# A linear-attention and feed-forward kernel on one core: later units start one item later, and the third unit's scans go between the first scores and the first row

## The chip, the cores and the metric

One core of a Trainium2 chip. Time is device microseconds (us) of one execution; the figure compared is the median over runs. Engines: TensorE (PE, with its weight loads as PEld), VectorE (DVE), ScalarE (ACT), GpSimd (POOL), and SyncE (SP), which issues the DMAs. A line such as L600 is a line of the kernel.

## The reference

Gated linear attention over 768 time steps for 4 batches of 8 heads of 48 channels, then a feed-forward layer on the 3072 tokens it yields. The weights come as float64, the rest as float32; the output is float32.

```python
state = np.zeros((B, H, D, D), dtype=np.float32)          # B, H, S, D = 4, 8, 768, 48
for t in range(S):
    state = alpha[:, :, t, :, None] * state + np.einsum('bhd,bhe->bhde', k[:, :, t], v[:, :, t])
    y[:, :, t] = np.einsum('bhd,bhde->bhe', q[:, :, t], state)
...
x = y.transpose(0, 2, 1, 3).reshape(B * S, H * D)         # 3072 x 384
h = x @ w_in                                              # 384 x 2048
g = np.maximum(0.01 * h, h)
return (g @ w_out).astype(np.float32)                     # 2048 x 384
```

## The kernel before

**Attention.** Time is cut into 6 chunks of 128 steps; a *unit* is one chunk of one batch, with all 8 heads (24 units, numbered 0 to 23). Per unit: `scans` turns alpha on VectorE (`e`, a transpose), takes running products along time (`up`, four scans), their reciprocals at every 16th step and a backward scan (`down`); `scaled_q` and `scaled_k` turn q and k and multiply them by these (`qs`, `ks`); `sum_up` sums the absolute values of `up` and `down` on ScalarE. Then on TensorE: `scores` (ks against qs, L465 a<-qs,ks), `past` (state against qs, L465 a or ph<-qs,small), `values` (masked scores against v, L465 <-sm,small), `products` (new state, L465 a<-small,ktok), and `k_tokens` (four transposes, L398). `mask_scores` copies one half of the scores to `sm` on ScalarE (L384) and masks it on POOL, the other half is masked on VectorE; `split` writes the result as a high and a low float32r part into `large`; `next_state` updates the state.

**Feed-forward.** Three units make a block of 384 tokens, so there are 8 blocks i. The hidden width is cut into 16 tiles f. An *item* n is a pair (i, f); items 0 to 31 alternate between blocks 0 and 1 (item 2f + i), and from item 32 the blocks 2 to 7 follow one after another, 16 items each. I write in(n) for the first product of item n (`ffn_in`, nine matmuls into a PSUM tile `ph`, L600) and out(n) for its second (`ffn_out`, nine matmuls into `a` or `b`, L629). out(n) is issued behind in(n+3). Between them stand t(n), the scaled copy on ScalarE (L605) and the maximum on VectorE (L608); gh(n), a rounded copy on ScalarE (L610); gl(n), the rest, on VectorE (L614). The weights come as 64-bit words; during items 0 to 28 `converting` makes each of the 16 weight tiles w0 to w15 (a high and a low part) with six VectorE steps and two on ScalarE.

**What sets the order.** A scheduler places instructions by their order in the program and by its own estimate; three things bind it. VectorE's and ScalarE's work on items and on units from 9 on is chained in the order of emission (`put`). Each matmul emitted by `multiply` with `row`, and each product once `row` is set, is chained to the last one (`in_row`). And PSUM and SBUF buffers are reused as the scheduler hands them out, so that a matmul can wait for whoever read its bank last.

**The two phases.** `attention` does units 0 to 8 at the start. Units 9 to 23 are the *later units*: `attention_later` is a generator of steps, and `pace` advances it while the items run, twice per item (a call before and one after t): each call adds `slices` to `due` and emits steps until `emitted` has reached it. A unit's preparation has 7 steps: e; the four scans; reciprocal and backward scan; q turned; qs; k turned; ks. *row(u)* is the chained group past(u), scores(u+1), values(u), products(u); with mask, split, state and a unit's preparation a unit has 11 steps. Steps 1 to 28 are the start (units 9 and 10, of 11 the preparation). Step 15 (14 emitted) is held back while block 1's sums still stand in PSUM.

Items in the trace: at 149.07 us TensorE starts out(27), behind in(29); at 167.56 us in(35), at 195.79 us row(10).

Of the kernel before, what the change touches and what calls it, by code (L numbers as in the profile page):

```python
# [23 lines left out]
def gated_linear_attn_ffn(ctx, tc, q, k, v, alpha, w_in, w_out, out):  # L24
# [9 lines left out]
    NF = DF // P  # L34
# [25 lines left out]
    LAG = 3  # L60
    SOON, EARLY = 2, 3
    SL = 11 * UPB
    FIRST, LEAD = 29, 14


    kinds = ["a", "b"]
# [1 line left out]
    def bank(tag=None):  # L68
        if tag is None:
            tag = kinds[0]  # L70
            kinds.append(kinds.pop(0))
        return ps_x.tile([P, 512], F32, name=tag)
# [205 lines left out]
    def banks4():  # L278
        return bank().rearrange("r (p n) -> r p n", p=NP)
# [86 lines left out]
    def scores(u):  # L366

        pe, qs, ks = live[u]
        ss = [banks4(), banks4()]
        M = C if u < AHEAD else HB  # L370
        for p in range(NP):
            for s, lo in ((0, 0), (1, HB)):
                for t in range(0, C, M):
                    yield ss[s][t:t + M, p, :], ks[lo:lo + D, p, t:t + M], qs[lo:lo + D, p, :], True, True
        live[u].append(ss)
# [36 lines left out]
    def past(u):  # L412

        tb, b = units[u]
        qs, W = live[u][1], state[b].rearrange("r p n -> r (p n)")
        if u < AHEAD:
            y = banks4()
            ys[u] = [y[:, s::2, :] for s in (0, 1)], y
        else:
            first = bank()  # L420
            full = [first, ps_h.tile([P, 512], F32, name="ph")]
            ys[u] = [t[:, 0:2 * C].rearrange("r (p n) -> r p n", p=2) for t in full], first[:, 2 * C:2 * C + NP * D]
        if tb:
            for q, s, lo, top, p, at in heads():
                r = slice(0, BR) if u < AHEAD else slice(lo, lo + D)
                c, m = p * BR + lo, D if top else HB
                yield ys[u][0][s][at:at + m, q, :], W[r, c:c + m], qs[r, p, :], q == 0 and (s == 0 or u >= AHEAD), False

    def values(u):

        tb, b = units[u]
        V = vals_sb[u % NV]
        for q, s, lo, top, p, at in heads():
            c = (2 * p + s) * D
            m = D if top else HB
            yield (
                ys[u][0][s][at:at + m, q, :], V[:, c:c + m], masked[u][s][:, p, :],
                not tb and q == 0 and s == 0, q == 1 and (s == 1 or u >= AHEAD),
            )
        del masked[u]  # L440

    def products(u):

        tb, b = units[u]
        pe, qs, ktok = live[u][:3]
        V = vals_sb[u % NV]
        kv = None
        if tb < NC - 1:
            kv = ys[u][1] if u >= AHEAD else bank()[:, 0:NP * D]
            kv = kv.rearrange("d (p e) -> d p e", p=NP)  # L450
            for p in range(NP):
                for s, lo, m in ((0, 0, HB), (1, HB, D)):
                    h = 2 * p + s
                    yield kv[lo:lo + m, p, :], ktok[:, p, lo:lo + m], V[:, h * D:(h + 1) * D], True, True
        load_values(u + NV)
        live[u] = pe, kv

    row = []

    def multiply(groups, row=None):  # L460

        for group in groups:
            for out, weights, moving, start, stop in group:
                with tc.issue_after(row[-1].ins) if row else nullcontext():
                    made["product",] = nc.tensor.matmul(out, weights, moving, start=start, stop=stop, skip_group_check=True)  # L465
                if row is not None:
                    row[:] = [made["product",]]
# [79 lines left out]

    def attention_later(first, last):

        def prepared(u, at=None):  # L550

            if u < last:
                yield from chain(scans(u), scaled_q(u), scaled_k(u))
                sum_up(u)

        yield from prepared(first)
        for u in range(first - 1, last):
            new, old = u + 1 < last, u >= first
            next_one = prepared(u + 2)
            if not old:  # L560
                yield from next_one
            groups = [past(u)] if old else []
            if new:
                groups.append(scores(u + 1))
            if old:
                groups += [values(u), products(u)]
            multiply(groups, row)
            yield
            if old:
                yield from islice(next_one, 1)  # L570
                split(u)
                if u % UPB == UPB - 1:
                    gather(u // UPB)
                    ready.add(u // UPB)
                yield
            if new:
                mask_scores(u + 1)
                yield
            if old:
                next_state(u)  # L580
            if new:
                k_tokens(u + 1)
            yield
            yield from next_one

    def in_row():

# [2 lines left out]
    def ffn_in(i, f, steps=None):  # L590

        ordered = steps is not None
        first, second = steps or ((), ())
        xh, xl = xs[i]
        ph = ps_h.tile([P, 512], F32, name="ph")[:, 0:TB]
        n = 0
        with in_row():
            for g in range(NG):
                for wn, xt in ((HIGH, xh), (HIGH, xl), (LOW, xh)):
                    product = nc.tensor.matmul(ph, w_in_of(f, wn, g), xt[:, g, :], start=n == 0, stop=n == 3 * NG - 1)  # L600
                    n += 1
        if row or i > 1:
            row[:] = [product]
        t = ffp.tile([P, TB], F32, name="t")
        put(ordered, "ACT", lambda: nc.scalar.mul(t, ph, 0.01))  # L605
        for step in first:
            next(step, None)
        put(ordered, "DVE", lambda: nc.vector.tensor_tensor(t, ph, t, ALU.max))  # L608
        gh = ffp.tile([P, TB], F32R, name="gh", bufs=LAG + 1)
        put(ordered, "ACT", lambda: nc.scalar.copy(gh, t))  # L610
        for step in second:
            next(step, None)
        gl = ffp.tile([P, TB], F32R, name="gl", bufs=LAG + 1)
        made["gl", i, f] = put(ordered, "DVE", lambda: nc.vector.tensor_tensor(gl, t, gh.bitcast(F32), ALU.subtract))  # L614
        return gh, gl
# [49 lines left out]
    for n, _ in enumerate(st):  # L665
        if n == 2:
            load_values(NV - 1)
        while LOADS and LOADS[0][0] in made:
            key, f, part = LOADS.pop(0)
# [3 lines left out]
        u = AHEAD - EARLY + converted  # L673
# [4 lines left out]
        if n in STARTS:  # L678
            i, f = items[len(gs)][:2]
# [5 lines left out]
    due, emitted = 0.0, 0  # L685
    new = coming = None
    later_units = attention_later(AHEAD, NU)

    def pace(slices):

        nonlocal due, emitted
        while True:
            due += slices
            while emitted < due and not (1 in pos and emitted == 14):
                next(later_units, None)
                emitted += 1
            yield

    steady = None
    for n in range(len(items) + LAG):  # L700
        if n < len(items):
            i, f, slices, _ = items[n]
            if f == 0:
                while i not in ready:
                    next(later_units)
            if n == FIRST:
                steady = pace((SL + LEAD) / (2 * (2 * NF + NF - FIRST)))
            elif i > 2 and f == 0:
                due, emitted = 0.0, 0
                steady = pace(SL / (2 * NF))  # L710
            if loaded_f < NF:
                load_weights(loaded_f)
                loaded_f += 1
                if loaded_f == NF:
                    asked, later = later, None
                    with behind("raw", NF - 1):
                        for fn, *args in asked:
                            fn(*args)
            pump = (steady,) if steady else ()
            if n < len(STARTS):  # L720
                pass
            elif i == 0:
                if coming is None:
                    coming = converting(f + SOON, True)
                    next(coming)
                old, new, coming = new or iter(()), coming, converting(f + SOON + 1, True)
                gs[n] = ffn_in(i, f, (pump, (coming, new, old, new) + pump))
            elif i == 1:
                gs[n] = ffn_in(i, f, ((new, new) + pump, (new,) + pump))
                next(new, None)  # L730
            else:
                gs[n] = ffn_in(i, f, (pump, pump))
        if n >= LAG:
            i, f, _, tag = items[n - LAG]
            ffn_out(i, f, gs.pop(n - LAG), tag)
# [135 lines left out]
```

## Time and profile before

| | us |
|---|---|
| median of 3 runs (528.07 to 528.47) | 528.27 |
| the profiled execution, its time | 526.68 |
| its span, first to last instruction | 525.0 |

| stretch of the span, us | TensorE busy, us | VectorE busy, us | granted clock |
|---|---|---|---|
| 0 to 60: attention, units 0 to 8 | 55.02 | 53.68 | 1.00 |
| 60 to 150: items of blocks 0 and 1, weights made | 90.00 | 89.43 | 1.00 |
| 150 to 180: last items of block 1, units 9 and 10 begin | 25.16 | 24.18 | 0.89 |
| 180 to 216: block 2, units 10 to 12 | 35.32 | 26.83 | 1.00 |
| 216 to 500: blocks 2 to 7, units to 23 | 284.00 | 179.84 | 1.00 |
| 500 to 525: the end | 20.12 | 6.67 | 0.99 |

A row's busy time is against the stretch's length: between 60 and 500 us TensorE falls short of full in two stretches only, 4.8 us in the third and 0.7 us in the fourth. The granted clock is the share of TensorE's full clock. In rows of the timeline the columns are start, us, engine, line, operation, out<-in, shapes, count, and in brackets the idle time before it and what ended that; a start to start distance is what an operation costs in a row of them, its own duration overlaps the next.

### The profile page before, as it was taken

What the parts mean: (1) busy time and instruction counts of PE and PEld (TensorE: products, weight loads), DVE (VectorE), ACT (ScalarE), POOL (GpSimd) and SP (SyncE); (2) the same over time, 40 slices, a digit from 0 to 9 for tenths busy, and PEclk for the clock granted to TensorE, in tenths of its full rate; (3) what the DMA queues carried; (4) which work ended last, traced back from release to release, by engine and by line L of the source; (5) the groups of instructions that cost most, each with busy time, mean ns of one, the idle gap of its engine ahead of it and who ended that gap; (6) DMA issues with size and microseconds to landing.
All of it is one profiled execution on the core that took longest, in us unless ns stands there. A gap on an engine that the chain in (4) does not pass through costs nothing.

```text
span 525.0 us, 10767 instructions
## 1 busy us (share of the span) xinstructions
PE 509.6 (97%) x4178; PEld 489.5 (93%) x4178; DVE 380.6 (73%) x710; ACT 235.7 (45%) x504; POOL 71.6 (14%) x143
## 2 busy tenths in 40 slices
PE   8998999999989799999999999999999999999996
PEld 7787899999989799899999999999999999999996
DVE  6999999999999387687586686686685783333331
ACT  2775755555525343444443553444443452334331
POOL 4565500000000101111111110102101010000000
PEclk9999999999999799999999999999999999999999
DMA  9999974446715412523322421433412011001001
GB/s 145 168 187 187 229 180 122 120 122 162 169 29 153 118 43 58 120 70 92 83 57 66 125 75 42 109 69 89 99 43 52 2 46 24 1 1 45 1 0 51
DMA packets 92985, 46.68 MB, mean 89 GB/s; under 512 B 57856, under 2 KB 90112, under 8 KB 92928
## 3 DMA queue, kind: packets, MB, share of 16 engines
q1 hardware_dynamic: 92928, 45.93, 40.0%
q8 instruction: 35, 0.57, 0.5%
q14 instruction: 22, 0.18, 0.1%
HBM read 38.83 MB, written 4.72 MB: 83 GB/s over the span
## 4 chain that ended last, share of the span: by engine, by line
PE 69%; DVE 18%; DMA 5%; issue 4%; SPq 1%; ACT 1%; DVEq 0%; ACTq 0%
PE b L629 28%; PE ph L600 26%; PE a L465 8%; DVE pw L265 3%; DVE bits L263 2%; DVE bits L254 2%; DMA raw<-in_moe_w_in_dram 2%; DVE gl L614 2%; PE ph L465 2%; DMA small<-in_alpha_dram 2%; DVE t L608 2%; PE b L287 1%; PE b L465 1%; DVE pw L261 1%; DVE bits L251 1%
## 5 line engine op out<-in xcount | busy, mean ns | idle before, releaser
L600 PE MATMUL ph<-large,w 128*128 128x384 f32 x1152 | 224.7, 336 | 2.1 <-DVE t L608 2.0
L600 PEld LDWEIGHTS ph<-large,w 128*128 128x128 f32 x1152 | 200.4, 188 | 4.7 <-DVE t L608 3.0
L629 PE MATMUL b<-w,gh 128*128 128x384 f32 x672 | 168.2, 337 | 0.0
L608 DVE TENSOR_TENSOR t<-ph,t 128x384 f32<-128x384 f32 x128 | 70.6, 551 | 102.5 <-ACT t L605 102.2
L605 ACT ACTIVATE t<-ph 128x384 f32<-128x384 f32 x128 | 62.5, 488 | 136.8 <-PE ph L600 136.5
L629 PEld LDWEIGHTS b<-w,gh 128*128 128x128 f32 x672 | 119.7, 188 | 1.3 <-issue 0.5
L629 PE MATMUL b<-w,gl 128*128 128x384 f32 x336 | 108.0, 335 | 0.0
L610 ACT CAST gh<-t 128x384 fp32r<-128x384 f32 x128 | 65.7, 513 | 91.7 <-DVE t L608 91.6
L614 DVE TENSOR_TENSOR gl<-t,gh 128x384 fp32r<-128x384 f32 x128 | 70.8, 553 | 20.5 <-ACT gh L610 20.1
L629 PEld LDWEIGHTS b<-w,gl 128*128 128x128 f32 x336 | 62.7, 188 | 0.0
L385 POOL TENSOR_SCALAR_AFFINE_SELECT sm<-sm 128x512 f32<-128x512 f32 x33 | 25.0, 768 | 128.5 <-ACT sm L384 110.2
L335 POOL COPY small<-up 128x4 f32<-128x4 f32 x15 | 4.6, 304 | 208.5 <-DVE up L276 208.5
L465 PE MATMUL a<-qs,ks 48*64 48x128 f32 (+1 forms) x552 | 27.6, 280 | 1.4 <-DVE ks L276 0.7
L465 PEld LDWEIGHTS a<-qs,ks 48*64 48x64 f32 (+1 forms) x552 | 23.6, 145 | 2.9 <-issue 0.9
L384 ACT COPY sm<-a 128x512 f32<-128x512 f32 x24 | 14.0, 583 | 14.9 <-PE b L465 12.3
L276 DVE TENSOR_TENSOR_SCAN up<-e,small 128x128 f32<-128x128 f32 x60 | 20.4, 402 | 0.1
L629 PE MATMUL a<-w,gh 128*128 128x384 f32 x96 | 20.2, 334 | 0.0
L276 DVE TENSOR_TENSOR_SCAN down<-e,small 128x511 f32<-128x511 f32 x15 | 19.2, 1283 | 0.9
L391 POOL TENSOR_TENSOR small<-small 48x192 f32<-48x192 f32 x32 | 18.5, 578 | 1.2
L257 ACT CAST w<-bits 128x768 fp32r<-128x768 f32 x16 | 13.4, 837 | 9.3 <-DVE bits L254 8.6
L276 DVE STREAM_TRANSPOSE e<-small 128x512 f32<-128x512 f32 x15 | 17.2, 1145 | 0.0
L629 PEld LDWEIGHTS a<-w,gh 128*128 128x128 f32 x96 | 17.0, 188 | 0.0
(106 smaller groups left out, 576.8 us busy)
## 6 DMA issues: line engine op xcount, KB each, us to landing
raw<-in_moe_w_out_dram SPq DMA_DIRECT2D x16, 384.0 KB, 4.1
small<-in_v_dram SPq DMA_DIRECT2D x24, 192.0 KB, 4.0
raw<-in_moe_w_in_dram SPq DMA_DIRECT2D x32, 144.0 KB, 4.3
out_dram<-o SPq DMA_DIRECT2D x24, 192.0 KB, 1.9
small<-in_alpha_dram SPq DMA_DIRECT2D x32, 96.0 KB, 2.3
small<-in_q_dram SPq DMA_DIRECT2D x30, 96.0 KB, 2.2
small<-in_k_dram SPq DMA_DIRECT2D x30, 96.0 KB, 2.2
small<-in_alpha_dram SPq DMA_DIRECT2D x30, 80.0 KB, 2.2
```

The costliest lines, as they stand in the source:

```text
L265: put(ordered, "DVE", lambda: nc.vector.scalar_tensor_tensor(rest, low.bitcast(U32), 2.0 ** -52, rest, ALU.mult, ALU.mult))
L276: return put(u >= AHEAD, "DVE", lambda: op(*args))
L384: made["sm", u] = nc.scalar.copy(sm[s], ss[s])
L385: made["mask", u] = nc.gpsimd.affine_select(out=sm[s], in_=sm[s], compare_op=ALU.is_ge, fill=0.0, base=0, pattern=[[0, NP], [1, C]], chann ...
L391: nc.gpsimd.tensor_tensor(*scalings.pop(0))
L465: made["product",] = nc.tensor.matmul(out, weights, moving, start=start, stop=stop, skip_group_check=True)
L600: product = nc.tensor.matmul(ph, w_in_of(f, wn, g), xt[:, g, :], start=n == 0, stop=n == 3 * NG - 1)
L605: put(ordered, "ACT", lambda: nc.scalar.mul(t, ph, 0.01))
L608: put(ordered, "DVE", lambda: nc.vector.tensor_tensor(t, ph, t, ALU.max))
L610: put(ordered, "ACT", lambda: nc.scalar.copy(gh, t))
L614: made["gl", i, f] = put(ordered, "DVE", lambda: nc.vector.tensor_tensor(gl, t, gh.bitcast(F32), ALU.subtract))
L629: product = nc.tensor.matmul(po[j], gt[:, js], w_out_of(f, wn), start=f == 0 and n == 0, stop=f == NF - 1 and n == 2)
```

## The change

Four edits, all on the later units and on TensorE's order:

```diff
-    FIRST, LEAD = 29, 14
+    FIRST, LEAD = 30, 14
...
     def attention_later(first, last):
-        def prepared(u, at=None):
+        def prepared(u):
             if u < last:
                 yield from chain(scans(u), scaled_q(u), scaled_k(u))
                 sum_up(u)
-        yield from prepared(first)
+        yield from chain(prepared(first), prepared(first + 1))
         for u in range(first - 1, last):
             new, old = u + 1 < last, u >= first
-            next_one = prepared(u + 2)
-            if not old:
-                yield from next_one
-            groups = [past(u)] if old else []
-            if new:
-                groups.append(scores(u + 1))
             if old:
-                groups += [values(u), products(u)]
-            multiply(groups, row)
-            yield
-            if old:
-                yield from islice(next_one, 1)
+                multiply([past(u)] + [scores(u + 1)] * new + [values(u), products(u)], row)
+                yield
+                if u > first:
+                    coming = prepared(u + 2)
+                    yield from islice(coming, 1)
                 split(u)
                 ...
-                yield
+            else:
+                multiply([scores(first)], row)
+                coming = prepared(first + 2)
+            yield
             ...
             yield
-            yield from next_one
+            yield from coming if old else islice(coming, 3)
...
         (ffn_in)
-        if row or i > 1:
+        if row or 2 * f + i >= FIRST:
             row[:] = [product]
...
             if n == FIRST:
-                steady = pace((SL + LEAD) / (2 * (2 * NF + NF - FIRST)))
+                steady = pace(1.0)
+            elif i == 2 and f == 0:
+                steady = pace((SL + LEAD - emitted) / (2 * NF))
```

The first step of unit 9 comes in item 30, not 29. Items 30 and 31 emit one step per call (four in all, from 1.24 a call); from item 32 the other 43 of 47 are spread over 32 calls, 1.344 each. The three scan steps of unit 11 come behind the first scores (step 15) and ahead of row(9), which is step 21 instead of 18; row(10) is step 29 in both, its last step before it ks(11), step 28. TensorE's chain begins at item 30 instead of with the first scores or block 2.

TensorE, from in(29) to in(32) (w_1748 is tile 14, w_1811 tile 15, w_663 tile 0; `a` belongs to block 1, `b` to block 0). Before:

```order
L600 MATMUL ph<-large,w_1748 128x384 x9
L629 MATMUL a<-w_1685,gh 128x384 x6
L629 MATMUL a<-w_1685,gl 128x384 x3
L600 MATMUL ph<-large,w_1811 128x384 x2
L629 MATMUL b<-w_1748,gh 128x384 x6
L600 MATMUL ph<-large,w_1811 128x384 x7
L629 MATMUL b<-w_1748,gl 128x384 x3
L600 MATMUL ph<-large,w_1811 128x384 x9
L600 MATMUL ph<-large,w_663 128x384 x9
```

After (to the first of out(28)):

```order
L597 MATMUL ph<-large,w_1748 128x384 x9
L597 MATMUL ph<-large,w_1811 128x384 x9
L626 MATMUL a<-w_1685,gh 128x384 x2
L626 MATMUL a<-w_1685,gl 128x384
L626 MATMUL a<-w_1685,gh 128x384 x2
L626 MATMUL a<-w_1685,gl 128x384
L626 MATMUL a<-w_1685,gh 128x384 x2
L626 MATMUL a<-w_1685,gl 128x384
L597 MATMUL ph<-large,w_1811 128x384 x9
L626 MATMUL b<-w_1748,gh 128x384 x2
```

in(30) now stands directly behind in(29) and ahead of out(27); in(31) and in(32) no longer stand side by side, out(28) comes between them.

VectorE in the same place, from the last step on tile 15 on (t_1956 is t(29), gl_1935 gl(28); e, up, down, qs are unit 9's; a scan is called SCALAR_TENSOR_TENSOR here, TENSOR_TENSOR_SCAN in the timeline). Before:

```order
L268 TENSOR_TENSOR w15_1811<-pw_1901,bits_1812 128x768
L614 TENSOR_TENSOR gl_1935<-t_1929,gh_1932 128x384
L276 STREAM_TRANSPOSE e_1958<-small_73 128x4x4x32
L276 SCALAR_TENSOR_TENSOR up_1960<-e_1958,small_73 128x128 x4
L608 TENSOR_TENSOR t_1956<-ph_1946,t_1956 128x384
L276 MEMSET e_1958 128x32
L276 RECIPROCAL small_73<-up_1960 128x32
L276 SCALAR_TENSOR_TENSOR down_1961<-e_1958,small_73 128x511
L614 TENSOR_TENSOR gl_1978<-t_1956,gh_1967 128x384
L276 STREAM_TRANSPOSE qs_2001<-small_73 128x4x4x32
```

After:

```order
L268 TENSOR_TENSOR w15_1811<-pw_1901,bits_1812 128x768
L611 TENSOR_TENSOR gl_1935<-t_1929,gh_1932 128x384
L605 TENSOR_TENSOR t_1956<-ph_1946,t_1956 128x384
L611 TENSOR_TENSOR gl_1961<-t_1956,gh_1959 128x384
L276 STREAM_TRANSPOSE e_1984<-small_73 128x4x4x32
L605 TENSOR_TENSOR t_1982<-ph_1972,t_1982 128x384
L276 SCALAR_TENSOR_TENSOR up_1989<-e_1984,small_73 128x128 x4
L611 TENSOR_TENSOR gl_1995<-t_1982,gh_1987 128x384
L276 MEMSET e_1984 128x32
L276 RECIPROCAL small_73<-up_1989 128x32
L276 SCALAR_TENSOR_TENSOR down_1990<-e_1984,small_73 128x511
```

t(29) and gl(29) now come ahead of unit 9, and unit 9's steps each stand about one elementwise pair later.

TensorE, from in(35) (w_1023, tile 3) to the start of row(9), whose first matmuls are a<-qs,small and ph<-qs,small. Before:

```order
L600 MATMUL ph<-large,w_1023 128x384 x9
L465 MATMUL a<-qs,ks 64x128 x16
L398 MATMUL a<-small,ks 128x112 x4
L465 MATMUL a<-qs,small 64x128
L465 MATMUL a<-qs,small 48x128
L465 MATMUL ph<-qs,small 64x128
```

After (the rest up to row(9) is in(36), out(33) and in(37)):

```order
L597 MATMUL ph<-large,w_1023 128x384 x9
L465 MATMUL a<-qs,ks 64x128 x16
L626 MATMUL b<-w_663,gh 128x384 x2
L626 MATMUL b<-w_663,gl 128x384
L398 MATMUL a<-small,ks 128x112 x4
L626 MATMUL b<-w_663,gh 128x384 x2
L626 MATMUL b<-w_663,gl 128x384
L626 MATMUL b<-w_663,gh 128x384 x2
L626 MATMUL b<-w_663,gl 128x384
L597 MATMUL ph<-large,w_1041 128x384 x9
L626 MATMUL b<-w_803,gh 128x384 x2
```

out(32), in(36), out(33) and in(37) now stand between the scores of unit 9 and row(9).

VectorE ahead of row(10) (t_2417 is t(39) and t_2455 t(40) before; t_2406 is t(39) and t_2448 t(40) after; ks is unit 11's). Before:

```order
L608 TENSOR_TENSOR t_2417<-ph_2407,t_2417 128x384
L276 STREAM_TRANSPOSE ks_2427<-small_73 128x4x4x32
L276 TENSOR_TENSOR ks_2427<-ks_2427,down_2354 128x512
L614 TENSOR_TENSOR gl_2434<-t_2417,gh_2425 128x384
L608 TENSOR_TENSOR t_2455<-ph_2445,t_2455 128x384
```

After:

```order
L605 TENSOR_TENSOR t_2406<-ph_2396,t_2406 128x384
L276 TENSOR_TENSOR qs_2417<-qs_2417,up_2287 128x512
L611 TENSOR_TENSOR gl_2427<-t_2406,gh_2420 128x384
L276 STREAM_TRANSPOSE ks_2450<-small_73 128x4x4x32
L605 TENSOR_TENSOR t_2448<-ph_2438,t_2448 128x384
L276 TENSOR_TENSOR ks_2450<-ks_2450,down_2288 128x512
```

ks(11) moves from ahead of t(40) to behind it. From the transposes behind row(11) on, the order of TensorE and VectorE is the same in both.

## Prediction

> **What bounds the kernel now.** I read the page first, then TensorE's waits, then the granted clock in narrow windows, then TensorE and VectorE in order of time.
>
> ```profile
> PE 509.6 (97%) x4178; PEld 489.5 (93%) x4178; DVE 380.6 (73%) x710; ACT 235.7 (45%) x504; POOL 71.6 (14%) x143
> ...
> PE ph L465 <- ACT sm L384: 2.3, 1, 2.3
> PE ph L600 <- DVE t L608: 2.0, 2, 1.6
> ```
>
> TensorE is busy 97% of the span, so only its waits can be won back, and the two largest are above (us in total, times, longest). The windows show what the granted clock does around the first, and what TensorE does undisturbed:
>
> ```profile
> 172.00:173.00 1.00, 0.00 (x0) 0.00 (x0) 0.99 (x2) 0.73 (x2) 0.00 (x0) 0.88 0.79 252
> 173.00:174.00 1.00, 0.00 (x0) 0.00 (x0) 0.63 (x2) 0.54 (x2) 0.00 (x0) 0.50 0.81 240
> 179.00:180.00 1.00, 1.00 (x15) 0.91 (x12) 0.00 (x0) 0.55 (x2) 0.00 (x0) 0.71 0.49 119
> 216.00:500.00 284.00, 284.00 (x2313) 277.35 (x2312) 179.84 (x346) 116.93 (x259) 28.52 (x53) 1.00 0.24 58
> 450.00:500.00 50.00, 50.00 (x290) 50.00 (x289) 17.88 (x33) 17.34 (x36) 0.00 (x0) 1.00 0.04 12
> ```
>
> The third number from the end of a row is the granted clock (0.88, 0.50, 0.71, 1.00, 1.00). It falls to one half at 172.76 (0.88 of one us) and is back at 179.58. From 216 us on TensorE waits for nothing (284.00 of 284.00). Undisturbed, 290 large products take 50 us: 0.172 each, 1.56 for nine. Now TensorE's places in order of time:
>
> ```profile
> 149.07 1.20 PE L629 MATMUL a<-w,gh 128*128 128x384 f32 x6
> ...
> 157.76 1.83 PE L600 MATMUL ph<-large,w 128*128 128x384 f32 x9 [1.59 <-DVE t L608]
> ...
> 167.56 1.73 PE L600 MATMUL ph<-large,w 128*128 128x384 f32 x9
> 169.22 1.10 PE L465 MATMUL a<-qs,ks 48*64 48x128 f32 x32
> ...
> 171.34 0.43 PE L465 MATMUL a<-qs,small 48*64 48x128 f32 x4 [0.48 <-DVE t L608]
> 174.10 0.47 PE L465 MATMUL ph<-qs,small 48*64 48x128 f32 x2 [2.33 <-ACT sm L384]
> 179.57 0.62 PE L629 MATMUL b<-w,gh 128*128 128x384 f32 x2
> ...
> 184.37 0.55 PE L398 MATMUL a<-small,ks 112*128 112x112 f32 x4
> 184.68 1.82 PE L600 MATMUL ph<-large,w 128*128 128x384 f32 x9
> 186.34 0.51 PE L629 MATMUL b<-w,gh 128*128 128x384 f32 x2
> ...
> 195.79 0.32 PE L465 MATMUL a<-qs,small 48*64 48x128 f32 x2
> 196.27 1.05 PE L465 MATMUL a<-qs,ks 48*64 48x128 f32 x32
> 197.26 0.43 PE L465 MATMUL a<-sm,small 128*64 128x128 f32 x4
> 198.72 0.62 PE L629 MATMUL b<-w,gh 128*128 128x384 f32 x2
> ```
>
> I write in(n) and out(n) for the first and second large product of item n, t(n), gh(n), gl(n) for its three elementwise results. 149.07 is out(27), directly behind in(29); 157.76 is in(32), 167.56 in(35); 169.22 the scores of unit 9; 171.34 to 179.57 row(9), which is the past of unit 9, the scores of unit 10, the values and products of unit 9; 179.57 is out(32), 186.34 out(34); 195.79 to 198.72 is row(10). The scores of unit 9 and row(9) stand side by side with only four transposes between, so row(9) meets the unevacuated scores. From 169.22 to 179.57 pass 10.35 us. The same work elsewhere: scores 0.99 (196.27 to 197.26), transposes 0.31 (184.37 to 184.68), a whole row 2.93 (195.79 to 198.72), 4.23 in all. 6.1 us are lost there: 2.8 waiting, 2.5 of a row that took 5.47 (174.10 to 179.57) instead of 2.93 at half clock, and small pieces. The two waits for t at in(31) and in(32), 2.0 together, come on top.
>
> **What the change does, part by part.** After it the scores keep their place (behind in(35)), but row(9) comes two items later, behind in(37). That takes away the wait for the mask and its half clock. What is late next is VectorE, which is never idle there:
>
> ```profile
> 149.47 0.55 DVE L608 TENSOR_TENSOR t<-ph,t 128x384 f32<-128x384 f32 x1
> 149.94 0.95 DVE L268 TENSOR_TENSOR w<-pw,bits 128x768 fp32r<-128x768 f32 x1
> 150.80 0.55 DVE L614 TENSOR_TENSOR gl<-t,gh 128x384 fp32r<-128x384 f32 x1
> 151.27 1.09 DVE L276 STREAM_TRANSPOSE e<-small 128x512 f32<-128x512 f32 x1
> 152.46 1.37 DVE L276 TENSOR_TENSOR_SCAN up<-e,small 128x128 f32<-128x128 f32 x4
> ...
> 161.04 1.10 DVE L276 STREAM_TRANSPOSE e<-small 128x512 f32<-128x512 f32 x1
> 161.99 0.54 DVE L614 TENSOR_TENSOR gl<-t,gh 128x384 fp32r<-128x384 f32 x1
> ...
> 172.00 0.56 DVE L614 TENSOR_TENSOR gl<-t,gh 128x384 fp32r<-128x384 f32 x1 [0.72 <-ACT gh L610]
> 172.48 0.68 DVE L276 TENSOR_TENSOR sm<-a,small 128x512 f32<-128x512 f32 x1
> 173.08 0.55 DVE L608 TENSOR_TENSOR t<-ph,t 128x384 f32<-128x384 f32 x1
> ```
>
> These are t(28), the last step on weight tile 15, gl(28), the first step of unit 9, and at the end gl(34), the mask of unit 9 and t(35).
>
> 1. *TensorE's order from item 30.* in(30) now follows in(29) at once. It needs t(28), which ends at 150.02, and the low half of tile 15, ending at 150.89; in(29) is issued by 149.07. TensorE stands some 1.5 us there, where out(27) stood before. The pay: out(28) comes between in(31) and in(32), and t(29) is no longer behind unit 9's first two steps, so both waits above go. By 166 us TensorE is about 1 us ahead, and this ahead is worthless if VectorE is not.
>
> 2. *VectorE's order.* From gl(28) to t(35) passed 173.08 - 150.80 = 22.28 us. After, the same operations stand there but for the mask (0.60, 172.48 to 173.08), which comes behind t(35); the idle 0.72 goes; a new 0.66 comes, since gl(29) now directly follows t(29) and has to go through ScalarE (183.53 to 184.66 below, 1.13 against 0.47). A transpose followed by what reads it takes 1.19 (151.27 to 152.46), followed by something else 0.95 (161.04 to 161.99); there are three such pairs before, one after: 0.5 less. t(35) starts at 150.80 + 22.28 - 0.60 - 0.72 + 0.66 - 0.5 = 171.9 and ends at 172.45. Bounds: 171.2 if ScalarE's detour hides, 173.0 if nothing is saved.
>
> 3. *The stretch to out(34).* The last six products of out(32) accumulate in a bank that t(35) frees, so TensorE goes on from 172.5 whatever it gained before: six products, in(36), out(33), in(37), 33 x 0.1733 = 5.7, row(9) 2.93, and 0.2 for two changes between small and large products (184.68 to 186.34 is 1.66, not 1.56): out(34) starts at 181.3. Before, 186.34, less 0.31 for transposes that now come later: 186.03. Gain 4.7. Mask, scores copy and the copy of the keys have 6 us of products to hide behind; without that cover they cost the 2.33 again.
>
> 4. *Unit 11's steps.* Its scans come between the first scores and row(9), its keys' product (ks) stays the last step before row(10). But the pace is another: 4 steps by item 32, then 43/32 = 1.344 per call, two calls an item. The 17th call reaches 26.8, the 18th 28.2, so step 28 (ks) and step 29 (row(10)) both come in the second call of item 40, and ks(11) stands behind t(40). Before, it came a call earlier, in item 39. The rows for that path:
>
> ```profile
> 181.24 1.72 PE L600 MATMUL ph<-large,w 128*128 128x384 f32 x9
> 183.53 0.56 DVE L608 TENSOR_TENSOR t<-ph,t 128x384 f32<-128x384 f32 x1 [6.88 <-ACT t L605]
> 184.00 0.41 DVE L276 TENSOR_TENSOR large<-ph,large 112x256 fp32r<-112x256 f32 x1
> 184.66 0.56 DVE L614 TENSOR_TENSOR gl<-t,gh 128x384 fp32r<-128x384 f32 x1
> ...
> 211.84 0.32 PE L465 MATMUL a<-qs,small 48*64 48x128 f32 x2
> 212.38 0.66 DVE L276 TENSOR_TENSOR ks<-ks,down 128x512 f32<-128x512 f32 x1
> 213.19 1.10 PE L465 MATMUL a<-qs,ks 48*64 48x128 f32 x32 [0.68 <-DVE ks L276]
> 215.69 0.62 PE L629 MATMUL b<-w,gh 128*128 128x384 f32 x2
> ```
>
> From the start of nine products to VectorE's slot behind t it is 2.76 (181.24 to 184.00); ks adds 0.7; TensorE has done nine products and the past by 1.65 + 0.48 = 2.13. Wait at row(10): 1.3 to 1.4, take 1.37; lower bound the 0.68 that such a wait costs at 213.19, upper the 2.33 of the longest wait shown.
>
> 5. *Row(11)* took 215.69 - 211.84 = 3.85, 0.92 over 2.93, waiting for ks(12). It now stands an item later, behind in(45), with ks(12) in item 44: 0.9 gained.
>
> 6. At nothing: the loads of unit 12 that now alternate with the outputs on SP's queue are needed only behind row(10), which ends at 198.72 now; the swapped places on POOL precede the same mask. From row(12) on the order is the same.
>
> Sum: -4.7 + 1.37 - 0.9 = -4.25 us on a span of 525.0. The profiled execution took 526.68, 1.59 under the median of 528.27; I carry the difference to the median: 524.0.
>
> **Clock.** The trace halves the clock after 0.48 and 2.33 us of waiting within 3 us, among small products. It keeps full clock through the 1.59 at 157.76. The new waits (about 1 to 1.5 at in(30), 2 in three pieces between 169 and 172.5, 1.37 inside row(10)) lie between. [...]
>
> **Rivals.** (a) The clock falls again, at the scores or inside row(10). For it: small products and waits mixed, as at 171 to 174. Against: no single wait reaches 2.33. Price: the 2.5 of before, so 526.5, still faster. (b) VectorE is nearer to TensorE than I take it, and row(10) waits only 0.68 or t(35) comes at 171.2: 0.7 each: 522.6; and if t(35) is done before TensorE asks, its own 1 us ahead counts too: 521.6. (c) The stall only moves: VectorE, with unit 11's scans now ahead of row(9), stays so late that in(38) and in(39) wait. They have some 3 to 4 us of room by the sum above, so VectorE must slip over 3 us more; then 4 us are eaten and it is no change, 528. Against: VectorE's idle 6.88 at 183.53. (d) Slower: the wait for a key product behind its t recurs in each of the 11 rows that follow row(11) and hold a unit's scores, as would be if the later pace kept the two steps in one call. At 1.37 each it is over the gain from the fourth row on (4 x 1.37 = 5.5), and 11 of them end at 539. Against: the count is set anew at item 48, the steps emitted by then are 47 in both, and the rows after 216 us wait for nothing now (above).
>
> **Numbers.** The sum as forecast 0.55 (522.7 to 525.4: t(35) by 0.8 either way, row(10) by 0.7); (a) 0.20; (b) 0.12; (c) 0.07; (d) 0.06. The range 521.8 to 526.8 holds the first three but for their edges. A change under 0.2% (1.06 us) can't be told from none here. Faster: 0.55 + 0.20 + 0.12 less an edge, 0.86; same 0.08; slower 0.06.
>
> **What would show it.** No wait of TensorE for sm L384; no 0.50 in the granted clock; a wait for t at in(30); large products between the scores of unit 9 and row(9); waits between 168 and 173 for t; a wait of about 1.4 for ks at row(10), none at row(11); out(34) at about 181.3. Wrong if the clock shows 0.50 anywhere after 60 us, or if TensorE waits at later rows.

## The result, and the profile after

The changed kernel takes 523.63 us (median of 4 executions, 523.46 to 524.25) against 528.37 for the kernel before (4 executions): ratio 0.9913, 95% interval 0.9896 to 0.993. Its profiled execution took 523.46 us, span 521.7. The forecast was 524.0.

TensorE's waits in the page of the changed kernel (L597 is in(n), L626 out(n), L605 t(n) on VectorE; only those of the later units and of the items are kept):

```profile
PE a L465 <- DVE ks L276: 1.5, 2, 1.3
PE a L465 <- DVE t L605: 1.0, 1, 1.0
PE ph L597 <- DVE t L605: 0.8, 1, 0.8
...
PE b L626 <- DVE t L605: 0.6, 1, 0.6
...
PE ph L597 <- DVE w L268: 0.2, 1, 0.2
```

The 2.3 for `sm` and the 2.0 for `t` at two products are gone; in their place stand 1.0, 0.8, 0.6 and 0.2, and the 1.27 for ks(11) (in the first row; the rest of it belongs to the first 60 us). The windows, at the same places as before:

```profile
172.00:173.00 1.00, 0.58 (x3) 0.58 (x4) 0.37 (x1) 1.00 (x4) 0.00 (x0) 1.00 0.74 224
173.00:174.00 1.00, 1.00 (x8) 1.00 (x7) 0.91 (x2) 0.64 (x3) 0.38 (x1) 1.00 0.78 207
...
216.00:500.00 284.00, 284.00 (x2314) 277.35 (x2313) 180.12 (x345) 116.56 (x258) 30.00 (x53) 1.00 0.23 58
```

The granted clock stays at 1.00 where it was 0.88 and 0.50, and from 216 us on TensorE again waits for nothing. TensorE in order of time:

```profile
147.82 1.75 PE L597 MATMUL ph<-large,w 128*128 128x384 f32 x9
150.40 0.62 PE L597 MATMUL ph<-large,w 128*128 128x384 f32 x2 [0.83 <-DVE t L605]
151.27 1.50 PE L597 MATMUL ph<-large,w 128*128 128x384 f32 x7 [0.24 <-DVE w L268]
...
169.33 1.10 PE L465 MATMUL a<-qs,ks 48*64 48x128 f32 x32 [0.95 <-DVE t L605]
172.42 0.61 PE L626 MATMUL b<-w,gh 128*128 128x384 f32 x2 [0.58 <-DVE t L605]
173.59 1.72 PE L597 MATMUL ph<-large,w 128*128 128x384 f32 x9
...
178.37 0.32 PE L465 MATMUL a<-qs,small 48*64 48x128 f32 x2
...
180.75 0.62 PE L465 MATMUL a<-small,ktok 128*48 128x48 f32 x16
181.30 0.62 PE L626 MATMUL b<-w,gh 128*128 128x384 f32 x2
...
191.30 0.32 PE L465 MATMUL a<-qs,small 48*64 48x128 f32 x2
...
193.23 1.10 PE L465 MATMUL a<-qs,ks 48*64 48x128 f32 x32 [1.27 <-DVE ks L276]
...
195.73 0.62 PE L626 MATMUL b<-w,gh 128*128 128x384 f32 x2
...
214.34 0.62 PE L465 MATMUL a<-small,ktok 128*48 128x48 f32 x16
...
515.85 0.34 PE L626 MATMUL b<-w,gl 128*128 128x384 f32 x1
```

In order: in(29); in(30) in two pieces, behind t(28) and then tile 15's low half; the scores of unit 9; out(32) behind t(35); row(9), now at 178.37 with large products ahead of it; out(34) at 181.30; row(10) from 191.30, with its wait for ks(11); the state products of row(11); the last large product. VectorE's chain:

```profile
151.13 0.55 DVE L611 TENSOR_TENSOR gl<-t,gh 128x384 fp32r<-128x384 f32 x1
...
152.73 0.56 DVE L611 TENSOR_TENSOR gl<-t,gh 128x384 fp32r<-128x384 f32 x1 [0.58 <-ACT gh L607]
...
171.79 0.58 DVE L605 TENSOR_TENSOR t<-ph,t 128x384 f32<-128x384 f32 x1
```

These are gl(28), gl(29) and t(35). The last large product of the kernel before is

```profile
519.78 0.34 PE L629 MATMUL b<-w,gl 128*128 128x384 f32 x1
```

**One ruler for all traces.** The first 150 us differ by up to 2.5 us between traces, so I measure from gl(28), at which VectorE is the busy engine. Marks: the state products (`a<-small,ktok`) of row(9) and of row(11), and the last large product. Before: 150.80, 178.59, 215.14, 519.78; after: 151.13, 180.75, 214.34, 515.85. From gl(28) to the last product: 368.98 before, 364.72 after, 4.26 less. The forecast's sum was 4.25. Row(11) stands one item (3.12 us) later after, so its two neighbouring columns are compared only together.

| kernel | gl(28) to row(9)'s products | on to row(11)'s | on to the last product | in all | gl(28) at | last product to end of span |
|---|---|---|---|---|---|---|
| before | 27.79 | 36.55 | 304.64 | 368.98 | 150.80 | 5.22 |
| after | 29.62 | 33.59 | 301.51 | 364.72 | 151.13 | 5.85 |
| e1_order | 24.84 | 36.12 | 304.63 | 365.59 | 151.97 | 6.14 |
| e4_steps | 30.77 | 29.88 | 304.64 | 365.29 | 151.48 | 6.33 |
| e2_noorder | 28.65 | 33.62 | 301.52 | 363.79 | 152.38 | 6.13 |
| e3_side | 26.45 | 37.67 | 301.52 | 365.64 | 153.29 | 6.27 |
| a_again | 29.60 | 33.61 | 301.52 | 364.73 | 151.32 | 5.85 |
| e7_fill | 26.27 | 36.11 | 304.63 | 367.01 | 151.59 | 5.50 |
| e5_key | 29.82 | 32.83 | 301.51 | 364.16 | 152.00 | 5.94 |
| e8_all | 29.99 | 32.83 | 301.52 | 364.34 | 151.26 | 6.00 |

The mean granted clock is on record for every execution, not only for the profiled one. Of 43 executions of the kernel before beside the experiments (two chips, median 528.38), one reached 0.997 and 30 were at 0.993 or below. Of the 10 executions of the changed kernel all were at 0.997 or above.

This mean holds the end of the program too. In eight of the ten traces the clock is lower at the end, where TensorE has nothing left to do (before: one half from 524.33 us; after: from 518.69; means of 0.90 to 0.93 over 500 to 530 us in e1 to e4, of 0.90 and 0.92 over 515 to 520 in a_again and e5); in e7 and e8 it is at 1.00 from 500 to 520. The mean over the span is 0.996 to 0.999 in the nine traces other than the one before; in those of after, e1, e2, e3 and e4 (0.996 to 0.998) the clock is at 1.00 up to 500 us, so there the end alone makes the difference. In the trace before, the 6.82 us at half clock in the middle take 0.0065 more off it (half of 6.82 us on a span of 525.0). So I read a mean of 0.995 or below as a fall elsewhere too (40 of the 43 are there); this is an estimate from the means of these ten traces, and it doesn't say where the clock fell.

### The profile page after: what moved, and what is told of

Its sections match the earlier page's. It is cut to its first block, busy times and chain, and to the rows that moved or that the text cites. A ratio compares the mean times of both kernels' runs of the same rounds, so it can differ in the third digit from the quotient of the medians.

```text
span 521.7 us, 10758 instructions
## 1 busy us (share of the span) xinstructions
PE 507.4 (97%) x4178; PEld 487.6 (93%) x4178; DVE 380.4 (73%) x710; ACT 236.0 (45%) x504; POOL 75.9 (15%) x143
## 4 chain that ended last, share of the span: by engine, by line
PE 72%; DVE 16%; DMA 5%; issue 3%; SPq 2%; ACT 1%; DVEq 0%; ACTq 0%
PE b L626 29%; PE ph L597 28%; PE a L465 8%; DMA raw<-in_moe_w_in_dram 3%; DVE pw L265 2%; DVE bits L254 2%; DVE bits L263 2%; PE b L465 2%; DVE gl L611 2%; DVE t L605 2%; PE ph L465 1%; DVE bits L251 1%; PE a L398 1%; PE b L287 1%; DVE pw L261 1%
## 5 line engine op out<-in xcount | busy, mean ns | idle before, releaser
L597 PE MATMUL ph<-large,w 128*128 128x384 f32 x1152 | 224.5, 336 | 1.1 <-DVE t L605 0.8
L597 PEld LDWEIGHTS ph<-large,w 128*128 128x128 f32 x1152 | 200.6, 188 | 3.4 <-DVE t L605 1.1
L626 PE MATMUL b<-w,gh 128*128 128x384 f32 x672 | 168.9, 338 | 0.6 <-DVE t L605 0.6
L605 DVE TENSOR_TENSOR t<-ph,t 128x384 f32<-128x384 f32 x128 | 70.6, 552 | 98.5 <-ACT t L602 98.1
L626 PEld LDWEIGHTS b<-w,gh 128*128 128x128 f32 x672 | 119.6, 188 | 2.2 <-DVE t L605 0.8
L626 PE MATMUL b<-w,gl 128*128 128x384 f32 x336 | 108.3, 335 | 0.0
L626 PEld LDWEIGHTS b<-w,gl 128*128 128x128 f32 x336 | 62.7, 188 | 0.0
L465 PE MATMUL a<-qs,ks 48*64 48x128 f32 (+1 forms) x552 | 26.3, 272 | 3.0 <-DVE ks L276 1.5
L465 PEld LDWEIGHTS a<-qs,ks 48*64 48x64 f32 (+1 forms) x552 | 22.4, 140 | 4.7 <-ACT gh L607 1.5
L626 PE MATMUL a<-w,gh 128*128 128x384 f32 x96 | 20.5, 334 | 0.0
L626 PEld LDWEIGHTS a<-w,gh 128*128 128x128 f32 x96 | 17.0, 188 | 0.0
```

What stands on the lines that cost most here:

```text
L626: product = nc.tensor.matmul(po[j], gt[:, js], w_out_of(f, wn), start=f == 0 and n == 0, stop=f == NF - 1 and n == 2)
```

## Experiments

The theory: the gain is the stall and the half clock at row(9), which go because row(9) no longer stands beside the scores of unit 9; VectorE sets the pace up to t(35). The rival: the order of TensorE fixed sooner, or the later start, carries the gain. All ratios are to the kernel before in the same runs (medians 528.28 on one chip for the first four, 528.45 on another for the rest).

**e1_order: the order alone, on the kernel before.**

```diff
-        if row or i > 1:
+        if row or 2 * f + i >= 30:
```

> The kernel before, with one line changed: TensorE's chain begins at item 30 instead of with the first scores. Everything else, VectorE's order too, is as before. Theory (the gain of the change is the stall and the half clock at row(9), and up to t(35) VectorE sets the pace): the two waits of 2.0 us at in(31) and in(32) become one of about 1 to 1.5 at in(30), TensorE comes to the scores of unit 9 up to 1 us earlier, and waits there or at row(9) that much longer for t or sm; the half clock stays. Median 527.9 to 528.6, no measurable gain. Rival (a good part of the gain comes from the order being fixed sooner): 1 to 2 us less, 526.4 to 527.4.

Median 526.06, ratio 0.9964 (0.9945 to 0.9984): a gain of 2.2, more than the rival's forecast too, and my expectation of none was wrong. TensorE at row(9), in this order first past, the copy's wait, the state products, out(32):

```profile
172.49 0.43 PE L465 MATMUL a<-qs,small 48*64 48x128 f32 x4 [0.47 <-DVE t L608]
174.44 0.32 PE L465 MATMUL ph<-qs,small 48*64 48x128 f32 x2 [1.52 <-ACT sm L384]
...
176.81 0.62 PE L465 MATMUL a<-small,ktok 128*48 128x48 f32 x16
177.36 0.62 PE L629 MATMUL b<-w,gh 128*128 128x384 f32 x2
```

It still waits for t and for sm, but 1.52 instead of 2.33, and in this execution the clock did not fall (1.00 in every window from 150 to 222 us): from 174.44 row(9) needs 2.92 us, not 5.47. That is 2.55 of the 3.39 it saves on the ruler. The other 0.8 is the copy to sm. VectorE is not faster: gl(28) to t(35) is 22.27 us (22.28 before). ScalarE's rows show the copy's place, first before, then here:

```profile
172.26 0.47 ACT L643 COPY o<-a 128x384 f32<-128x384 f32 x1
173.46 0.58 ACT L384 COPY sm<-a 128x512 f32<-128x512 f32 x1 [0.73 <-DMA out_dram<-o]
```

```profile
173.42 0.47 ACT L643 COPY o<-a 128x384 f32<-128x384 f32 x1
173.81 0.58 ACT L384 COPY sm<-a 128x512 f32<-128x512 f32 x1
```

Before, ScalarE stood 0.73 us, which the trace puts down to an output's DMA, and here not. A wait of this kind is not in the trace before alone: here the trace puts 1.06 us at the next copy to sm (176.61) down to an output's DMA. At the copy above e4 has none (173.28), and what brings it about was not settled. So the trace before held a term that I had counted as waiting for the mask. The 12 executions differ: four at a clock of 0.992 or 0.993 took 527.0 to 528.7, the other eight (0.995 and above) 525.4 to 526.5. By these means the clock still falls in part of them, but less often: nine of the 43 executions before reach 0.995. The wait at in(32) is gone, and at in(31) 0.29 is left:

```profile
155.46 1.83 PE L600 MATMUL ph<-large,w 128*128 128x384 f32 x9 [0.29 <-DVE t L608]
```

**e4_steps: the steps alone, on the kernel before** (its start, pace and order kept).

```diff
-    FIRST, LEAD = 30, 14
+    FIRST, LEAD = 29, 14
...
-        if row or 2 * f + i >= FIRST:
+        if row or i > 1:
...
-                steady = pace(1.0)
-            elif i == 2 and f == 0:
-                steady = pace((SL + LEAD - emitted) / (2 * NF))
+                steady = pace((SL + LEAD) / (2 * (2 * NF + NF - FIRST)))
```

(The diff is against the changed kernel.)

> The kernel before with the steps alone: three steps of unit 11 between the first scores and row(9). Start (item 29), pace and the start of TensorE's chain are as before. Row(9) then stands behind in(37), as in the changed kernel; row(10) and row(11) stay where they were in the kernel before. Theory (the steps alone take the stall at row(9) away; what is left of the edits is worth little): t(35) by 172.3 to 173.0 since the mask comes behind it, out(34) at 181.5 to 182.2 against 186.0, no half clock; row(10) may wait 0 to 1.3 for ks(11), row(11) keeps its 0.9. Median 523.8 to 525.3. Rival (the later start of unit 9 and the order are needed too: without them VectorE is too late): 526.5 to 528.4.

Median 524.65, ratio 0.9920 (0.9889 to 0.9952); on the ruler 365.29, that is 3.69 of the 4.26. Five of six executions are at 0.997 or above. The waits for t at in(31) and in(32), 2.0 in all, are still there and cost little, since VectorE is no later for them (t(35) stands 22.26 behind gl(28), before 22.28) and TensorE waits for t(34) inside the scores all the same:

```profile
172.00 1.09 PE L465 MATMUL a<-qs,ks 48*64 48x128 f32 x28 [1.64 <-DVE t L605]
```

Row(10) does not wait. The steps alone bring most of the change, as the theory has it. The parts do not add up, though: e1 and the next run show that the rest of the edits, without these steps, bring about half of it as well (2.2 and 2.4 us).

**e3_side: the changed kernel without these steps.**

```diff
-            yield from coming if old else islice(coming, 3)
+            yield from coming if old else islice(coming, 0)
```

> The changed kernel without the three steps of unit 11 between the first scores and row(9): row(9) is step 18 again, and in TensorE's order only out(32) and in(36) stand between scores(9) and row(9), not in(37) and out(33) as well. Theory (what costs is a row that meets scores not yet copied; about 3.1 us of products are now in between, with the wait for t(35) 3.7, and in the trace before row(9) had to wait until some 3.5 us behind the scores): the wait for sm is 0 to 0.7 us, no half clock, and row(10) and row(11) as in the changed kernel: median 523.5 to 524.5. Rival (the three steps carry the gain; one item between does not do): the wait for sm is back with over 1.5 us and the clock falls to one half, 526 to 528.

Median 525.91, ratio 0.9955 (0.9936 to 0.9973): between the two forecasts, and neither reason is whole. There is no wait for sm, as the theory had it: one item between scores and row is enough. But row(10) waits longer:

```profile
196.28 1.10 PE L465 MATMUL a<-qs,ks 48*64 48x128 f32 x32 [2.21 <-DVE ks L276]
```

Unit 11's scans now come behind row(9), and ks(11) is late by as much: 2.21 against 1.27, and the ruler has 0.92 more than after. This I missed: at this place the three steps earn by giving VectorE its work sooner, not by moving row(9). Four of the 12 executions are at 0.995 or below; this kernel has a wait of 2.2 us at row(10), but where their clock fell is not recorded.

**e2_noorder: the changed kernel without the order.**

```diff
-        if row or 2 * f + i >= FIRST:
+        if row or i > 1:
```

> The changed kernel with one line put back: TensorE's chain again begins with the first scores, so in(31) and in(32) stand side by side. Theory (VectorE sets when t(35) is done, so what TensorE gains before it is lost again at the scores or at out(32)): waits of about 1.5 at in(31) and in(32) come back, the waits for t at scores(9) and out(32) shrink by as much, row(9) at 178.4 plus 0 to 0.5 us; median 523.4 to 524.3. Rival (the order sooner fixed carries part of the gain): the waits add up, 525 to 525.7.

Median 524.65, ratio 0.9942 (0.9915 to 0.9969), between the two forecasts. On the ruler it is 0.93 us *better* than the changed kernel, which neither side expected. TensorE at the scores of unit 9 and at out(32):

```profile
168.21 0.44 PE L465 MATMUL a<-qs,ks 48*64 48x128 f32 x4
170.77 1.09 PE L465 MATMUL a<-qs,ks 48*64 48x128 f32 x28 [2.13 <-DVE t L605]
171.79 0.62 PE L626 MATMUL b<-w,gh 128*128 128x384 f32 x2
```

The waits at in(31) and in(32) did not come back: here unit 9's later start alone removes them, as in e1 the order alone did but for 0.29. TensorE waits 2.13 for t(34), and then out(32) runs through without waiting for t(35). In the built programs the reason is the bank: the second of out(32)'s three sums is put into the bank of in(35) in the changed kernel, and into one long free here. Yet the executions are slower than the ruler says: seven of nine are at 0.995 or below, five of them at 0.993 or below. The one profiled is at full clock up to its last product (1.00 in the windows up to 500 us, products at the full pace from there on), so where the others lose it is not shown; the wait of 2.13 us among small products is my guess. So the order costs 0.9 us on the ruler, and the changed kernel, which has it, is at 0.997 or above in all ten executions.

**a_again: the changed kernel once more,** beside the kernel before.

> The changed kernel itself, for the spread of its executions beside those of the kernel before on the same chip. Theory (the kernel before loses TensorE's full clock for a while in most of its executions and the changed kernel in few or none): nearly all executions with a mean granted clock of 0.997 or 0.998, median 523.3 to 524.3. Rival (its waits of 0.95 and 0.58 at scores(9) and out(32) lower the clock too in part of the executions): several of them at 0.993 to 0.995 and a median over 524.6.

Median 523.91, ratio 0.9920 (0.9902 to 0.9939); all six executions at 0.997 to 1.00; 364.73 on the ruler. These are the theory's numbers: with its waits no execution has a mean that points to a fall ahead of the end.

**e7_fill: work instead of waiting, on the kernel before.** Sixteen products whose sum is thrown away, ahead of row(9):

```diff
+            if u == first:
+                fill(16)
             multiply(groups, row)
...
+    def fill(count):
+        pos[2] = [bank("b")[:, 0:DM] for _ in range(UPB)]
+        for _ in range(count):
+            with in_row():
+                product = nc.tensor.matmul(pos[2][0], w_in_of(3, HIGH, 0), xs[2][0][:, 0, :], start=True, stop=True, skip_group_check=True)
+            row[:] = [product]
```

> The kernel before plus 16 large products (2.75 us at 0.172 each) between scores(9) and row(9), written to a bank that out(32) overwrites: TensorE works there instead of standing, and nothing else is changed. Theory (row(9) costs so much because the clock falls to one half during the stall): no half clock, row(9) takes 2.9 instead of 5.5 us, from gl(28) to the last product 366.4 us instead of 369.0 (365.6 if the output's DMA does not hold the mask's copy up), the spread of the executions gone, median 525.0 to 526.2. Rival (the clock falls for another reason, or the work added is paid in full): 528 to 531.

Median 526.37, ratio 0.9962 (0.9945 to 0.9979): 2.1 us less with 2.75 us more of work, against the rival's 528 to 531 and 0.2 above the theory's range. Eleven of 12 executions are at 0.997 or above, where one of 43 was. The spread is not gone (524.95 to 529.00), and the slowest is the twelfth, at 0.991.

```profile
172.11 3.05 PE L593 MATMUL b<-large,w 128*128 128x384 f32 x16 [1.02 <-DVE t L620]
175.00 0.55 PE L398 MATMUL a<-small,ks 112*128 112x112 f32 x4
175.48 0.32 PE L465 MATMUL a<-qs,small 48*64 48x128 f32 x2
...
177.86 0.62 PE L465 MATMUL a<-small,ktok 128*48 128x48 f32 x16
178.41 0.62 PE L641 MATMUL b<-w,gh 128*128 128x384 f32 x2
```

Row(9) takes 2.93 at full clock (175.48 to 178.41; 1.00 from 170 to 185 us). The ruler has 367.01, 0.6 above my 366.4: the added work had to wait 1.02 for t itself, and so it overshot the stall. So the half clock of the trace before goes with TensorE's standing there, though in e1 TensorE stood 0.47 and 1.52 at full clock: with large products in that place it does not come in this trace, and it was 2.5 of the 6.1 us lost. Whether the standing alone is enough, or the small products around it count too, these runs do not separate.

**e5_key: ks(11) a call earlier, on the changed kernel.**

```diff
-                steady = pace((SL + LEAD - emitted) / (2 * NF))
+                due = 4.5
+                steady = pace(1.325)
```

> The changed kernel with two numbers of the pace: at item 32 the count starts at 4.5, not 4, and advances 1.325 per call, not 1.344. Ks(11) then comes a call earlier than row(10), as in the kernel before; row(9), row(10) and row(11) keep their items. Theory (the wait of 1.27 at row(10) is only the place of ks(11) behind t(40)): the wait goes to 0 to 0.2, from gl(28) to the last product 363.4 to 363.7 instead of 364.7, median 522.2 to 523.0. Rival (VectorE is late there anyway, and one of the steps that now stand ahead of a t delays TensorE elsewhere): 523.4 to 524.5.

Median 524.14, ratio 0.9917 (0.9897 to 0.9938): no gain over the changed kernel that these runs can show, and within the rival's range.

```profile
170.72 1.09 PE L465 MATMUL a<-qs,ks 48*64 48x128 f32 x28 [1.14 <-DVE t L605]
...
193.52 1.10 PE L465 MATMUL a<-qs,ks 48*64 48x128 f32 x32 [0.49 <-DVE ks L276]
```

The wait at row(10) goes from 1.27 to 0.49, not to 0.2, and t(35) comes 0.24 later from gl(28) (20.90 against 20.66); 0.56 is left on the ruler. Three of six executions are at a clock of 0.994 and took 524.4 to 524.7, the other three 523.05 to 523.9. So, by these means, the clock falls in half of the executions of a kernel whose waits here are shorter or hardly longer than the changed kernel's (1.14, 0.30 and 0.49 against 0.95, 0.58 and 1.27); why is open. The place of ks(11) behind t(40) was most of that wait, not all.

**e8_all: e5 without the order, and with 13 such products ahead of the first scores.**

```diff
+                fill(13)
                 multiply([scores(first)], row)
```

> Three edits on the changed kernel: the pace of the run before (ks(11) a call earlier), TensorE's chain again from the first scores on, and 13 large products (2.2 us) put ahead of the first scores, into a bank that out(32) overwrites, so that TensorE works where it waited 2.13 us for t(34) without the chain. Theory (without the chain the products are 0.9 us nearer to the end, and it was only the clock that made such executions slower): from gl(28) to the last product 362.3 to 362.8 us, no half clock, median 521.3 to 522.3. Rival (the 2.2 us of work come on top, since the wait was for VectorE and it slips by as much, or the clock falls all the same): 523.5 to 525.5.

Median 523.41, ratio 0.9909 (0.9888 to 0.9930), the lowest median here, but within the spread of the changed kernel (523.63 and 523.91). All six executions are at 0.996 or above, which is what the clock's part of the theory asks for. The 521.3 to 522.3 do not come: the banks are handed out anew, out(32) again shares one with in(35), and waits:

```profile
172.94 0.62 PE L637 MATMUL b<-w,gh 128*128 128x384 f32 x2 [0.58 <-DVE t L616]
```

The ruler has 364.34. No version here beats the changed kernel by an amount that these runs can tell from none.

## Why the prediction was right, point by point

*What bounds the kernel.* Right: of 6.1 us that I called lost around row(9), 2.5 was the half clock. The row takes 2.92 in e1's trace and 2.93 in e7's, and in e7, with work in the place of the stall, the clock stays at 1.00 there. Of the 2.8 of waiting, 0.73 was ScalarE, by the trace behind an output, and not the mask itself; I had not read ScalarE's rows. And the product that waited 2.33 is one of past(9), which reads no scores: in the built program its bank is that of the first half of the scores of unit 9. So this wait, too, is for a bank.

*Step 1, the order from item 30.* The wait came out at 0.83 + 0.24 = 1.07, not 1.5. That TensorE would be some 1 us ahead by 166 us and gain nothing held: in(35) stands 15.52 behind gl(28) against 16.76. The two reasons given for the end of the two waits were not needed together: the order alone leaves 0.29 of them (e1), unit 9's later start alone nothing (e2), and without either they stay at 2.0 (e4).

*Step 2, VectorE.* t(35) stands 20.66 behind gl(28); the forecast had 21.1 (171.9 - 150.80). The new idle is 0.58, forecast 0.66. The rest of the 0.44 is in the six transposes of this stretch, start to start: 6.64 us before and 5.80 after, 0.84 saved where I had 0.5. One of them, of ks(10), took 1.25 before though its reader did not follow it (168.41 to 169.66), so my rule for the pairs was too simple. By the clock of the trace 171.79 against 171.9, because this trace is 0.33 later at gl(28).

*Step 3, to out(34).* 181.30 against 181.3, and row(9) waits for nothing; the gain there 186.03 - 181.30 = 4.73 against 4.7. Two small errors cancelled: the start 0.33 later, t(35) 0.44 nearer. The wait for t(35), from which I counted, is the scheduler's choice of a bank (e2, e8), not a need of the computation.

*Step 4, ks(11).* The wait is 1.27 against 1.37, but row(10) takes 4.43 (191.30 to 195.73), 1.50 over 2.93: its products around the wait cost 0.23 more. *Step 5.* Row(11) takes 2.94, without a wait, as said. *Step 6* and the clear rows behind 216 us: as said, which disposes of rivals (c) and (d). Rival (b): in part, by the 0.44 of step 2. Rival (a), the clock: in the trace after it is at 1.00 from 150 to 500 us, and no mean of the ten executions, all 0.997 or above, points to a fall there. By the letter, though, a sign of being wrong came true, "0.50 anywhere after 60 us": the clock is at one half from 518.69 us on, behind the last product, where it costs nothing. The sign should have ended there.

*The sum.* On the ruler the start of row(10) comes 4.82 sooner (44.99 behind gl(28) before, 40.17 after), row(10) takes 1.50 more, row(11) 0.91 less, and the rest is equal within 0.03: 4.26. The first is 0.12 better than the 4.7, the second 0.13 worse than the 1.37. That the sum fits to 0.01 is therefore luck; that each term fits to 0.13 is not.

*The weak step: "I carry the difference to the median".* I took the 1.59 between the profiled execution and the median to hold for both kernels; after, it is 0.17 (523.46 against 523.63). The sum of 4.25 became 4.26 on the ruler, but the profiled executions differ by only 3.22 and the medians by 4.74. The trace before reached gl(28) earliest of all ten, at 150.80 (the others 151.13 to 153.29), and had the shortest end, 5.22 (the others 5.50 to 6.33). Against the means of the other nine these are 1.0 and 0.8 us, enough for a profiled execution 1.6 to 1.7 below its median; as far as ten traces tell they are luck, not something that a kernel takes along. After, 0.33 at the start and 0.63 at the end were lost against it in the traces. The medians gained 0.5 more than the ruler; the clock does not explain that, since the profiled execution before, at 0.993, lost as much clock as the middle one of the 43. It stays open. Without the carry the forecast would have been 522.4, so that 524.0 lies so near is in part luck.

## What to carry to other kernels

When a chained small product needs what another engine has yet to evacuate, put large products between the two: here one item (3.1 us) was enough (no wait for sm in e3), and what the stall cost in the trace before was about as much half clock afterwards (2.5) as waiting (2.8). Compare two traces from a mark behind the start, and take the spread of the executions and their mean clock along, because one profiled execution may have a lucky start and end (1.0 and 0.8 us here). Before a wait is called the bound of an engine, look at the bank in which it waits: here another order handed the banks out anew (e2, e8), and a plan made on the old ones did not hold.

## What the runs showed of the hardware

- The mean clock differs between executions of one and the same program. The kernel before had 0.988 (530.95 us) to 0.997 (525.29 us) in its 43 executions beside the experiments. With waits of 0.95, 0.58 and 1.27 us it was at 0.997 or above in all of 10 executions; in kernels with one wait of 2.13 or 2.21 us it was below 0.996 in 7 of 9 and 4 of 12; but with waits of 1.14, 0.30 and 0.49 (e5) it was 0.994 in 3 of 6. So the longest wait does not decide it by itself. Where in those executions it fell is not recorded; in the profiled ones of e1, e2 and e3 it is at 1.00 up to 500 us, in that of e5 from 145 to 185 and from 500 to 515.
- The time from TensorE's last work to the half clock varies as well: behind the end of the last product (as the profile models it) the clock fell after 4.2 us before (520.12 to 524.33) and after 2.5 in the trace after (516.19 to 518.69); in e8 the window from 515 to 520 us, which reaches 4.1 behind it (515.94), is still at 1.00.
- In the trace before, the clock was at one half from 172.76 to 179.58 us. When it fell, TensorE had waited 0.48 and then 0.99 of the 2.33 (from 171.77 on), with small products between; it came back 5.48 after the wait had ended (174.10). Through the 1.59 ahead of in(32) it had stayed at 1.00, and in e1 it stayed there through 0.47 and 1.52 at row(9) itself.
- Added work shortened the kernel: 2.75 us of products with no use took 2.1 us off (526.37 against 528.45, e7).
- ScalarE, too, was held, by the trace by an output's DMA: 0.73 us ahead of the copy to sm before, 1.06 us ahead of one in e1, and 2.01 us at the last copies after,

```profile
517.73 0.48 ACT L640 COPY o<-b 128x384 f32<-128x384 f32 x1 [2.01 <-DMA out_dram<-o]
```

  a wait of 2.0 us seen at that copy in both traces of the changed kernel and in e5, and in no other. It did not set the end: kernels without it had ends as long (e1 6.14, e8 6.00). What does set the end between 5.2 and 6.3 us stays open.
